# A tuned convolution and feed-forward kernel: softmax pieces, bands and second matmuls of blocks 1 to 4 in another order, with the next block's convolution sooner

## The chip, the cores and the metric

The kernel runs on one core of a Trainium2 chip. The metric is device time in microseconds (us), the median of several executions. All runs told of here were in the fast state, with a granted TensorE clock (the share of full speed) of 0.998 to 1.0. Ratios are the mean time of one kernel's fast runs over the mean of the other's in the same rounds on the same chip, so they are not quite the ratio of the medians quoted; the interval beside a ratio is the 95% one.

## The reference, cut to what matters

```python
def _attn_ref(x, weight_gen):                       # x (8, 4096, 192), weight_gen (8, 4096, 8, 7)
    w = np.exp(weight_gen - max over the 7 taps);  w = w / sum over the 7 taps
    # each position and head: weighted sum of the 7 last positions of x (a causal convolution)
    return np.einsum('bshk,bskhg->bshg', w, x_unfolded).reshape(8, 4096, 192)

def _moe_ref(x, w_in, w_out):                       # x (32768, 192), w_in (192, 2048), w_out (2048, 192)
    h = np.maximum(x @ w_in, 0.0)
    return h * h @ w_out
```

The convolution's result is the input of the feed-forward part.

## The kernel before

The 32768 rows are worked through in blocks: blocks 0 and 1 have 512 rows, all others 1024. A string for each block, its plan, gives the order in which work is issued. One letter is one step:

- `u`, a unit: 6 matmuls of the first product into an h tile (PSUM), a relu on ScalarE into a t1 tile, a square on VectorE into a g tile. A block of 1024 rows has 16.
- `M`, one half of one quarter of the second product: 32 matmuls into the two o banks. The second half of a quarter is followed by a copy of one bank on ScalarE and an add of the other on VectorE.
- `C`, the convolution of the next block: 120 short matmuls into two h tiles, then two copies on ScalarE (y).
- `E`, `S`, `B`: an exp on ScalarE, a softmax piece on VectorE (total, reciprocal, four scalings), and a band on VectorE (a masked spread of the weights that the conv's matmuls read). The last piece of a part also issues the transfers that carry its rows to the bands. `L` loads weights.

```python
p_t1 = ctx.enter_context(tc.tile_pool(name="p_t1", bufs=5))
ps_h = ctx.enter_context(tc.tile_pool(name="ps_h", bufs=3, space=bass.MemoryType.PSUM))
ps_o = ctx.enter_context(tc.tile_pool(name="ps_o", bufs=1, space=bass.MemoryType.PSUM))
...
def st_unit(j, u):
    h = ps_h.tile([P, 2, TB], f32, name="h", tag="h")
    ...                                              # 6 matmuls
    t1 = p_t1.tile([P, 2, TB], f16, name="t1")
    nc.scalar.activation(out=t1, in_=h, func=ActF.Relu)
    g = p_g.tile([P, 2, TB], f16, name="g")
    nc.vector.tensor_tensor(out=g, in0=t1, in1=t1, op=AluOp.mult)
...
def st_conv(j):
    yps = [ps_h.tile([P, 2 * TB], f32, name="yp", tag="h") for _ in range(-(-NK // per))]
    ...                                              # 120 matmuls
...
def o_sum(j, qt, ccs, o):
    nc.scalar.copy(out=o_sb, in_=o[0][:, c])
    if len(o) == 2:
        nc.vector.tensor_tensor(out=o_sb, in0=o[1][:, c], in1=o_sb, op=AluOp.add)
...
steady = "MuMuuu" * 3 + "MuuuMCu"
plans = {
    0: "B1 X1 u u u E1 S1 u C u u u u",
    1: "L3 u u B2 M E2 B3 u M E2 u u S2 u M u C u S2 M",
    2: "L4 u u u E3 M u u u M B4 u u u u M B5 S3 u u u u M u E3 C u",
    3: "L5 L6 M S3 u u u M u u u u M u M B6 E4 u u u M M B7 u u S4 u E4 M u C M u",
}                                                    # from block 4 on: steady, with E, S, B filled in
```

The program issues work to every engine in this order, and the traces show it done in it: in the run with M C u below, ScalarE's copy was done at 75.90 us, and the add on VectorE that follows it began only at 77.83, after the softmax piece and the squares issued ahead of it. So a step's place fixes what stands ahead of it in each engine's queue. An h tile is one of 3, which the conv shares; a t1 tile is one of 5; the two o banks are there once.

The softmax here doesn't subtract the row's maximum and nothing guards it: scores larger than these inputs give would overflow.

## Time and profile before

| | before |
|---|---|
| median | 748.29 us (747.95 to 749.56, 4 runs); first measured as 748.35 (3 runs) |
| span of the traced run | 746.6 us |
| TensorE busy | 739.0 us |
| ScalarE, VectorE busy | 624.7, 621.8 us |
| matmuls | 15,106, each with its own weight load |

The busy line, the chain that ended last and the one wait of TensorE stand in the prediction below. Three more lines of the page are needed. The first is from the list of transfer queues (packets, MB, share of the 16 transfer engines' time), the others are the two costliest groups of matmuls (count, busy us, mean ns, then the idle time ahead of them and what ended it):

```profile
q8 instruction: 118, 1.93, 1.1%
...
L475 PE MATMUL o<-w_o,g 64*128 64x192 f16 (+1 forms) x8032 | 385.3, 243 | 0.9 <-DVE o_sb L491 0.6
...
L441 PE MATMUL h<-y,w_i 64*128 64x512 f16 (+1 forms) x3168 | 379.7, 370 | 2.2 <-ACT t L450 0.9
```

### The profile page before, as it was taken

To read this page: it belongs to the slowest core of one execution; us is meant where nothing else is said; L and a number is where in the kernel's file an instruction comes from. 1 tells how busy PE (TensorE), PEld (TensorE's weight loads), DVE (VectorE), ACT (ScalarE), POOL (GpSimd) and SP (SyncE) were. 2 spreads that over 40 slices of the span, in tenths; PEclk is the share of its full clock that TensorE was granted. 3 is DMA by queue.
4 is the path that set the end of the run, shared out by engine and by line. 5 is a ranking of instruction groups with operands and counts; after the bars stand their busy time and mean duration, and the time that the engine had idled before them with its cause. 6 is when DMAs were issued, how large, how long until landed. Compare 5 with 4: busy or idle time off the path is not lost.

```text
span 746.6 us, 33289 instructions
## 1 busy us (share of the span) xinstructions
PE 739.0 (99%) x15106; PEld 556.5 (75%) x15106; DVE 621.8 (83%) x1001; ACT 624.7 (84%) x755; POOL 88.8 (12%) x130
## 2 busy tenths in 40 slices
PE   8999999999999999999999999999999999999998
PEld 4767877877777777777777777787777777777787
DVE  5999998998889888888889888898888987677853
ACT  5998788888888888888888888888888888888874
POOL 7321220101101100011000110001100011001000
PEclk9999999999999999999999999999999999999999
DMA  8654454436554234644245542365441354441312
GB/s 223 112 106 109 80 101 85 100 70 139 94 118 79 75 57 80 140 79 73 45 74 139 102 65 53 51 139 108 59 80 48 57 108 80 60 73 51 51 46 65
DMA packets 122169, 64.81 MB, mean 87 GB/s; under 512 B 83849, under 2 KB 118636, under 8 KB 121516
## 3 DMA queue, kind: packets, MB, share of 16 engines
q1 hardware_dynamic: 77708, 45.66, 22.4%
q0 software_dynamic: 44176, 16.93, 20.5%
q8 instruction: 118, 1.93, 1.1%
q14 instruction: 23, 0.19, 0.1%
q10 hardware_dynamic: 144, 0.10, 0.0%
HBM read 48.61 MB, written 28.70 MB: 104 GB/s over the span
## 4 chain that ended last, share of the span: by engine, by line
PE 94%; DVE 2%; issue 1%; DMA 1%; ACT 1%; POOL 0%; DVEq 0%; ACTq 0%
PE o L475 45%; PE h L441 43%; PE yp L416 6%; DVE g L453 1%; DVE bd L348 1%; DMA wr<-v_first 0%; DMA wg<-in_weight_gen_dram 0%; POOL wr L330 0%; ACT t L450 0%; DVE v_first L239 0%; ACT ex L217 0%; DVE ssum L224 0%; DVE rcp L231 0%; DVE o_sb L491 0%; ACT y L427 0%
## 5 line engine op out<-in xcount | busy, mean ns | idle before, releaser
L450 ACT ACTIVATE t<-h 128x1024 f16<-128x1024 f32 x512 | 496.7, 1026 | 65.6 <-PE h L441 65.3
L453 DVE TENSOR_TENSOR g<-t 128x1024 f16<-128x1024 f16 x512 | 334.3, 687 | 100.5 <-ACT t L450 97.8
L475 PEld LDWEIGHTS <-g 64*128 64x128 f16 (+1 forms) x8032 | 352.3, 94 | 55.0 <-issue 4.8
L475 PE MATMUL o<-w_o,g 64*128 64x192 f16 (+1 forms) x8032 | 385.3, 243 | 0.9 <-DVE o_sb L491 0.6
L441 PE MATMUL h<-y,w_i 64*128 64x512 f16 (+1 forms) x3168 | 379.7, 370 | 2.2 <-ACT t L450 0.9
L441 PEld LDWEIGHTS <-w_i 64*128 64x128 f16 x3168 | 162.6, 94 | 117.2 <-issue 5.2
L348 DVE TENSOR_TENSOR bd<-wr,mask 128x4160 f16<-128x4160 f16 (+3 forms) x89 | 149.3, 1701 | 4.0 <-DMA wr<-v_first 4.0
L300 POOL DMA_DIRECT2D xt<-in_x_dram x62 | 51.2, 830 | 446.7 <-PE yp L416 423.7
L489 ACT COPY o_sb<-o 128x384 f32<-128x384 f32 x129 | 62.2, 482 | 33.8 <-PE o L475 33.8
L491 DVE TENSOR_TENSOR o_sb<-o,o_sb 128x384 f32<-128x384 f32 x123 | 68.2, 555 | 8.4 <-ACT o_sb L489 5.6
L427 ACT CAST y<-yp 128x1024 f16<-128x1024 f32 (+1 forms) x64 | 48.1, 803 | 14.5 <-PE yp L416 14.5
L416 PE MATMUL yp<-bd,xt 128*32 128x104 f16 (+8 forms) x3864 | 51.7, 208 | 0.3 <-DVE bd L348 0.2
L416 PEld LDWEIGHTS <-xt 128*32 128x32 f16 (+3 forms) x3864 | 46.2, 92 | 6.7 <-issue 6.2
L239 DVE TENSOR_TENSOR v_big<-ex,rcp 128x112 f16<-128x112 f32 (+1 forms) x136 | 27.3, 263 | 1.8 <-DMA vd<-v_big 0.6
L217 ACT ACTIVATE ex<-wg 128x448 f32<-128x448 f32 (+2 forms) x44 | 27.2, 618 | 1.8 <-DMA wg<-in_weight_gen_dram 1.8
L224 DVE TENSOR_REDUCE ssum<-ex 128x64 f32<-128x448 f32 (+2 forms) x44 | 26.1, 594 | 2.5 <-ACT ex L217 2.3
L231 DVE RECIPROCAL rcp<-ssum 128x64 f32<-128x64 f32 (+2 forms) x44 | 23.7, 539 | 1.5
L290 POOL DMA_DIRECT2D xt<-in_x_dram x7 | 3.8, 549 | 135.8 <-PE yp L416 135.8
L330 POOL DMA_DIRECT2D wr<-v_first x31 | 16.8, 561 | 16.3 <-DVE v_first L239 16.1
L539 PE MATMUL wp<-warm 128*128 128x512 f16 x39 | 11.4, 459 | 1.3 <-DVE warm L531 1.3
L539 PEld LDWEIGHTS <-warm 128*128 128x128 f16 x39 | 4.3, 114 | 7.6 <-issue 3.5
L239 DVE TENSOR_TENSOR v_first<-ex,rcp 128x112 f16<-128x112 f32 (+1 forms) x48 | 9.1, 255 | 0.3
(24 smaller groups left out, 28.2 us busy)
## 6 DMA issues: line engine op xcount, KB each, us to landing
out_dram<-o_sb SPq DMA_DIRECT2D x63, 384.0 KB, 3.0
xt<-in_x_dram POOLq DMA_DIRECT2D x42, 240.0 KB, 5.9
wg<-in_weight_gen_dram SPq DMA_DIRECT2D x4, 1064.0 KB, 8.3
xt<-in_x_dram POOLq DMA_DIRECT2D x20, 192.0 KB, 5.6
wr<-vd SPq DMA_DIRECT2D x38, 80.0 KB, 3.6
vd<-v_big SPq DMA_DIRECT2D x5, 512.0 KB, 5.5
wg<-in_weight_gen_dram SPq DMA_DIRECT2D x5, 392.0 KB
wg<-in_weight_gen_dram SPq DMA_DIRECT2D x3, 616.0 KB, 4.1
```

What stands on the lines that cost most here:

```text
L217: nc.scalar.activation(out=self.ex[:, lo:hi].rearrange("p r g k e -> p (r g) k e"), in_=self.wg[:, lo:hi].rearrange("p r (g e) k -> p (r g ...
L239: eng.tensor_tensor(out=bass.AP(tensor=v.tensor, offset=v.offset + lo * H * SL + lo % SL * 2 + g * SL * 2, ap=[list(v.ap[0]), [H * SL + 2, ...
L300: eng.dma_start(out=dst[:, first:last], in_=ap)
L348: nc.vector.tensor_tensor(out=bd_t[j][:, H * lo : H * (lo + len(tiles) * n)].rearrange("p (g m c) -> p g m c", g=shape[1], c=2 * SL), in0= ...
L416: nc.tensor.matmul(out=yps[k // per][p0 : p0 + m, col + a : col + b], lhsT=x_t[s][:, i, 32 * q : 32 * q + m], rhs=bd[:, h // 2, h % 2, a - ...
L427: nc.scalar.copy(out=y[:, k0:k1, 0:th], in_=yp[:, 0 : (k1 - k0) * th].rearrange("p (k c) -> p k c", c=th),)
L441: nc.tensor.matmul(out=h[:, half, jj * th : (jj + 1) * th], lhsT=w_in_chunk(u * per + jj, slot, half), rhs=y_t[j][r0 : r0 + RT, k, 0:th], ...
L450: nc.scalar.activation(out=t1, in_=h, func=ActF.Relu)
L453: nc.vector.tensor_tensor(out=g, in0=t1, in1=t1, op=AluOp.mult)
L475: nc.tensor.matmul(out=oo[:, cc * Dm : (cc + 1) * Dm], lhsT=g[r0 : r0 + n, cc * P : (cc + 1) * P], rhs=w_o[r0 : r0 + n, fc, :], start=(fc ...
L489: nc.scalar.copy(out=o_sb, in_=o[0][:, c])
L491: nc.vector.tensor_tensor(out=o_sb, in0=o[1][:, c], in1=o_sb, op=AluOp.add)
```

## The change

As the plans read, it moves softmax pieces and bands to other places in VectorE's order, moves the conv of the next block up in block 3, and spreads the halves of the second product around them. Plans 1 to 3 are rewritten, and block 4 gets a plan of its own. Nothing else changes; the set of instructions is the same.

```diff
-            1: "L3 u u B2 M E2 B3 u M E2 u u S2 u M u C u S2 M",
-            2: "L4 u u u E3 M u u u M B4 u u u u M B5 S3 u u u u M u E3 C u",
-            3: "L5 L6 M S3 u u u M u u u u M u M B6 E4 u u u M M B7 u u S4 u E4 M u C M u",
+            1: "L3 u u B2 M E2 B3 u M E2 u u S2 u M u S2 C u M",
+            2: "L4 u u u E3 S3 u B4 u B5 M E3 u u S3 M u u u M u u u u M u C M u",
+            3: "L5 L6 u u u M E4 B6 u u u M u M E4 B7 u u u M M S4 C S4 u M u u u M u u",
+            4: "B8 u E6 M u M S6 u u u u M u u M u B9 E5 u u M M u C M u u E5 u M S5 u",
```

## The prediction

Passages of the record are cut where marked: rules that it had not measured, and the hand-over times that it put beside the copy and the add. No term of its sum is among them; the sum came to +1.3, that is 749.6. Its 1.25 us for copy and add is an estimate: the trace of before shows 0.48 and 0.55, with 0.03 us from the last matmul's end to the copy, 0.03 from the copy to the add and 0.05 from the add to the next matmul, 1.14 in all. That a busy TensorE need not be at its pace shows in the same trace: it is busy for all of 36.8 to 56.3 us, and three units there take 2.05 us (from 36.82) against 1.94 later (from 56.27). That the 3 h tiles and 5 t1 tiles are "just" enough in the steady blocks is its judgement; the trace shows that TensorE waits for no engine from 150 to 740 us.

> **What bounds the kernel now.** I read the page first (busy shares, then the chain that ended last), then the TensorE timeline block by block, then who waited for whom between 24 and 150 us, then the timelines of VectorE (DVE) and ScalarE (ACT) for the blocks that change.

> The page's busy line and the chain's shares:
> ```profile
> PE 739.0 (99%) x15106; PEld 556.5 (75%) x15106; DVE 621.8 (83%) x1001; ACT 624.7 (84%) x755; POOL 88.8 (12%) x130
> PE 94%; DVE 2%; issue 1%; DMA 1%; ACT 1%; POOL 0%; DVEq 0%; ACTq 0%
> ```
> TensorE ends the run. A busy PE need not be at its pace, so I took start-to-start distances. From about 55 us on, one unit (st_unit, 6 matmuls) takes 0.65 us and one half of a second matmul (an "M" of the plan, 32 matmuls) 1.32 us, again and again; a conv ("C") takes 1.53 us. The last stretch of block 3 and the start of block 4, TensorE timeline (start, length, engine, group, count, idle before it):
> ```profile
> 73.99 1.59 PE L416 MATMUL yp<-bd,xt 128*32 128x104 f16 x120
> 75.52 1.49 PE L475 MATMUL o<-w_o,g 64*128 64x192 f16 x32
> 76.85 0.81 PE L441 MATMUL h<-y,w_i 64*128 64x512 f16 x6
> 77.57 0.24 PE L475 MATMUL o<-w_o,g 64*128 64x192 f16 x1
> 78.43 1.48 PE L475 MATMUL o<-w_o,g 64*128 64x192 f16 x31 [0.62 <-DVE o_sb L491]
> ```
> This is the one visible hole. Block 3 ends "M C M u" and block 4 begins with "M": only one unit stands between the half that finishes a quarter of the output and the half that starts the next quarter in the same two o banks. The second matmul should have started near 77.61 and starts at 78.43: 0.82 us lost. In the list of waits of 24 to 150 us it is the only wait of PE on another engine:
> ```profile
> PE o L475 <- DVE o_sb L491: 0.6, 1, 0.6
> ```
> Other losses in these blocks are small: the first M of block 5 takes 1.43 us to the next start instead of 1.32, and a half at 139.3 us takes 1.62, together 0.4. They are in block 5, which the diff doesn't touch. The plan of the change adds no instruction and drops none (16 units and 2 bands a block, the same exps, softmax pieces and halves in total), so **all that can be gained is about 0.8 us, perhaps 1.2, of 748**.

> [...]at 77.04 the copy of the o bank starts on ACT and takes 0.48, so the add on DVE could start at about 77.55, but it stands behind two squares (g) and starts at 77.83. So the place of each piece in the queue is what the change plays with. [...]The trace's 99% hides the pace, but it is constant. [...]in the steady blocks there are none (PE has no wait on another engine from 150 us to 740), so the rings of 3 h tiles and 5 t1 tiles are just enough there. Whether they are enough in the new block 2 is the question below.

> **The change part by part.** Durations from the VectorE and ScalarE timelines of before, as start-to-start steps: g 0.60, a softmax piece of 8 rows 1.99 (total 0.61, recip 0.55, four scales 0.83), one of 6 rows 1.65, a band 2.23 to 2.27, an add 0.47; on ACT a relu (t1) 0.91, an exp 0.54, a copy of o 0.45, the two y copies together 1.4. VectorE in block 1 to 2 before:
> ```profile
> 37.94 0.50 DVE L224 TENSOR_REDUCE ssum<-ex 128x48 f32<-128x336 f32 x1
> 39.59 1.89 DVE L453 TENSOR_TENSOR g<-t 128x1024 f16<-128x1024 f16 x3
> 42.28 0.69 DVE L453 TENSOR_TENSOR g<-t 128x1024 f16<-128x1024 f16 x1 [0.80 <-ACT t L450]
> 44.72 2.32 DVE L348 TENSOR_TENSOR bd<-wr,mask 128x4160 f16<-128x4160 f16 x1
> 49.36 2.35 DVE L348 TENSOR_TENSOR bd<-wr,mask 128x3328 f16<-128x3328 f16 x2
> 57.28 0.49 DVE L224 TENSOR_REDUCE ssum<-ex 128x48 f32<-128x336 f32 x1
> ```
> VectorE has 1.2 us to spare at 42 to 44 and then none until after 58.9.

> (1) Boundary of blocks 3 and 4. After the change one half of block 2's quarters moves into block 2 and block 3 ends "M u u", block 4 begins "u E6 M": three units, 1.94 us, instead of one. The copy [...] and the add [...] need about 1.25. **Saved: 0.82.**

> (2) Block 2. Both pieces S3 and both bands now stand within the first 7 units. TensorE's order starts at 36.82 as before. VectorE from 36.14, back to back: g, g 1.2; S2 1.65; g 0.6; three g 1.8; S3 1.99; g 0.6; B4 2.23; g 0.6; B5 2.27; then g of unit 6, 0.6: 13.54, so that this g ends at 49.7. The relu of unit 11 takes its t1 buffer (5 of them) and can't start before 49.7; unhindered it would start at about 48.85 (unit 11 ends at 36.82 + 5 units 3.35 + M 1.43 + 2 units 1.40 + M 1.43 + 3 units 2.05 + M 1.43 + 0.75 = 48.66). Its h buffer is then free at 50.75 and unit 14, which needs it, is due at 50.1. **Lost: about 0.7** (0.2 to 1.1, as the sum of 13.54 has small gaps either way and the band may wait for its rows). The rest of the block has room: second S3 piece ends at 52.0, relu 13 waits for a g of 52.5, just in time for the conv.

> (3) Block 3 and most of block 4. With adds at the head of the bands, each gap between a finishing half and the next starting half is two units and a conv or three units (1.94 to 2.2), and the ledger leaves 0.4 to 1.0 of margin at each: lost 0, up to 0.3. The conv five units sooner in block 3 gains nothing: conv is 1.53 us of TensorE wherever it stands, and its y was never waited for in the steady blocks.

> (4) Boundary of blocks 4 and 5. The new block 4 ends "C M u u E5 u M S5 u", and block 5 begins with "M". **This is the pattern of the old boundary 3/4 again**, one unit in between; the old block 4 ended "M C u" there, with 2.2 us. From the conv's start as zero: unit 13 is done at 3.6; ACT does relu 13 from 3.75, relu 14, exp (0.54), relu 15, to 7.0, then the copy to 7.4; TensorE has finished the half at 6.25 and wants the o banks at 6.87. The g of unit 15 (0.6) and the add (0.55) bring it to 8.2. **Lost: about 1.3** (0.6 if ACT and DVE are not behind, since copy and add alone need 1.25 against 0.65).

> (5) Behind it, S5's two pieces and S6 come within 6 us on VectorE in block 5; margin of the next add about 0: lost 0 to 0.2, say 0.1.

> Sum: -0.8 + 0.7 + 0 + 1.3 + 0.1 = +1.3, that is 749.6. I give some weight to the rivals and put it at 749.2.

> **Rivals.** First, the author's hope: the hole at 78.4 goes and nothing takes its place, 747.4. For it: that hole is the only recorded wait of PE; the total work is the same. Against: block 4's new end repeats the pattern, and the VectorE timeline shows no slack after 44 us in block 2. Second, only the hole moves (0.8 at 78 becomes 0.6 to 1.3 at the 4/5 boundary) and block 2 keeps pace: 748.1 to 748.9. For it: the five t1 buffers have carried a lag of some 3 us on VectorE before. Third, the pile-up in block 2 is worse: B4 and B5 also wait for the rows that S2 moves (before, issued from 39.7 and first read at 44.7; now both some 0.7 sooner), TensorE loses 1.5 in block 2, and the lag meets the adds in block 3: 750.5. For it: VectorE has 19.8 us of work in 20 us of block 2. Against: every lag of TensorE lets VectorE catch up, so it can't grow without end.

> **Range and chances.** The terms run from -0.8 + 0 + 0.6 = -0.2 to -0.8 + 1.1 + 0.3 + 1.4 + 0.2 = +2.2 about the median of 748.35, and the three times of before themselves spread by 1.3. So 747.6 to 750.6. Two per cent are 15 us, ten times any term: within 2% is all but certain.

> **What would show it.** Right: the TensorE timeline of after has no hole at the 3/4 boundary (about 79 us), a hole of 0.6 to 1.4 released by the DVE add at the first half of block 5 (about 102 us), and in block 2 (near 50 us) a unit that starts 0.2 to 1.1 late after a relu; all blocks from 6 on take as long as before. Wrong: no hole at 102, which would mean that ACT and DVE are further ahead at the end of block 4 than my ledger has them; or no delay in block 2; or a wait on a transfer, which I have at zero. A time under 747.5 would mean that the first rival holds; one over 751 that a lag carried through block 3 into several adds.

## The result

| | before | after |
|---|---|---|
| median | 748.29 us (4 runs) | 752.51 us (4 runs, 752.40 to 753.29) |
| ratio | | 1.0056 (1.0038 to 1.0073) |
| span of the traced run | 746.6 us | 750.7 us |
| matmul 566, early in block 2 | 37.27 us | 38.33 us |
| from there to matmul 2300 (called blocks 2 to 5; 2300 lies in block 5) | 88.47 us | 92.49 us |
| from there to matmul 15,000 | 611.82 us | 610.92 us |

The change costs 4.2 us. That is within 2%, as foretold, but outside the range of 747.6 to 750.6. The last three rows are worked out from the start times of matmuls with the same number, counted from 0, in both traces.

The busy line and the chain's shares of the page after:

```profile
PE 739.2 (98%) x15106; PEld 562.1 (75%) x15106; DVE 621.8 (83%) x1001; ACT 624.2 (83%) x755; POOL 90.7 (12%) x130
PE 90%; DVE 5%; DMA 1%; ACT 1%; issue 1%; POOL 0%; DVEq 0%; ACTq 0%
```

All engines have the same work. TensorE's part of the chain falls from 94 to 90%, VectorE's rises from 2 to 5%: TensorE has to wait. Its timeline after (start, length, engine, group, count, idle before it and what ended it), with the three new holes and the place where the old one was:

```profile
49.22 2.12 PE L441 MATMUL h<-y,w_i 64*128 64x512 f16 x18
52.56 0.82 PE L441 MATMUL h<-y,w_i 64*128 64x512 f16 x6 [1.22 <-ACT t L450]
...
55.49 1.58 PE L416 MATMUL yp<-bd,xt 128*32 128x104 f16 x120
57.00 1.32 PE L475 MATMUL o<-w_o,g 64*128 64x192 f16 x27
59.42 0.42 PE L475 MATMUL o<-w_o,g 64*128 64x192 f16 x5 [1.10 <-DVE g L453]
...
80.72 2.18 PE L441 MATMUL h<-y,w_i 64*128 64x512 f16 x18
82.66 1.56 PE L475 MATMUL o<-w_o,g 64*128 64x192 f16 x32
...
103.99 0.81 PE L441 MATMUL h<-y,w_i 64*128 64x512 f16 x6
105.25 0.24 PE L475 MATMUL o<-w_o,g 64*128 64x192 f16 x1 [0.45 <-ACT o_sb L489]
106.08 1.48 PE L475 MATMUL o<-w_o,g 64*128 64x192 f16 x31 [0.58 <-DVE o_sb L491]
```

- **Unit 14 of block 2** starts at 52.56, 1.38 us late (the distance between two matmuls, less the usual one; so are all losses below).
- **The half behind block 2's conv** stops after 27 of its 32 matmuls and goes on at 59.42, 1.30 us late. The prediction has nothing like it.
- **The boundary of blocks 3 and 4** is clean: three units in 1.94 us, then the half. The old hole of 0.81 is gone.
- **The start of block 5** has two holes, 0.61 and 0.78 us, for the two o banks.

Two smaller losses: 0.25 us at the fifth of the five units with which block 2 now begins, and 0.47 us in the half behind block 3's conv, again after its 27th matmul. The sum is 1.38 + 1.30 + 0.61 + 0.78 + 0.25 + 0.47 - 0.81 = 3.98, close to the 4.02 us by which blocks 2 to 5 grew. The 1.06 us at the start is tested below. The 0.90 won back later did not come again: in the second trace of the same code the last stretch took 612.85 us.

The list of waits for 24 to 150 us puts names to the holes:

```profile
PE h L441 <- ACT t L450: 1.2, 1, 1.2
PE o L475 <- DVE g L453: 1.1, 1, 1.1
...
PE o L475 <- DVE o_sb L491: 0.6, 1, 0.6
...
PE o L475 <- ACT o_sb L489: 0.5, 1, 0.5
```

For the hole before unit 14, VectorE's and ScalarE's timelines show what is behind it. VectorE:

```profile
43.01 0.61 DVE L224 TENSOR_REDUCE ssum<-ex 128x64 f32<-128x448 f32 x1
...
45.60 2.32 DVE L348 TENSOR_TENSOR bd<-wr,mask 128x4160 f16<-128x4160 f16 x1
...
48.43 2.35 DVE L348 TENSOR_TENSOR bd<-wr,mask 128x3328 f16<-128x3328 f16 x2
50.70 1.28 DVE L453 TENSOR_TENSOR g<-t 128x1024 f16<-128x1024 f16 x2
51.91 0.49 DVE L224 TENSOR_REDUCE ssum<-ex 128x48 f32<-128x336 f32 x1
```

ScalarE:

```profile
46.61 3.02 ACT L450 ACTIVATE t<-h 128x1024 f16<-128x1024 f32 x3
51.48 1.94 ACT L450 ACTIVATE t<-h 128x1024 f16<-128x1024 f32 x2 [1.85 <-DVE g L453]
54.33 1.94 ACT L450 ACTIVATE t<-h 128x1024 f16<-128x1024 f32 x2 [0.91 <-DVE g L453]
```

A softmax piece, square, band, square, band: only at 50.70 come the squares of units 6 and 7. The relu of unit 11 waits for the first of them to free its t1 tile, starts at 51.48, and unit 14 starts when it is done. By 58.45 VectorE has caught up; it then idles for 3.13 us, until 61.58.

For the stop at 59.42 the list names a square on VectorE. That looks wrong: the half reads the squares of units 1 to 8, and the eighth was done at about 54.2. Nor does a stop after 27 matmuls fit a square: each square is read by 4 matmuls of the half, so a wait for one would fall after 24 or 28. With the matmuls and their weight loads numbered in order, both 27-matmul stops of the trace, though a conv and some hundreds of instructions apart, lie at the same place of 256. Worked out from the trace's records:

```
stop at    number in stream   of 256   last packet of queue 8   TensorE goes on
 58.09          1726            190      56.69 to 57.97 us       59.42, 1.45 after it landed
 76.76          2494            190      74.63 to 75.78 us       77.28, 1.49 after it landed
```

So the theory to test was: in these two places TensorE had run out of instructions.

### The profile page after: what moved, and what is told of

Same layout as the page of the kernel before. It is cut to its first block, busy times and chain, and to the rows that moved or that the text cites. A ratio compares the mean times of both kernels' runs of the same rounds, so it can differ in the third digit from the quotient of the medians.

```text
span 750.7 us, 33286 instructions
## 1 busy us (share of the span) xinstructions
PE 739.2 (98%) x15106; PEld 562.1 (75%) x15106; DVE 621.8 (83%) x1001; ACT 624.2 (83%) x755; POOL 90.7 (12%) x130
## 4 chain that ended last, share of the span: by engine, by line
PE 90%; DVE 5%; DMA 1%; ACT 1%; issue 1%; POOL 0%; DVEq 0%; ACTq 0%
PE o L475 43%; PE h L441 41%; PE yp L416 6%; DVE g L453 2%; DVE bd L348 1%; DMA wr<-v_first 1%; DVE v_first L239 1%; ACT t L450 1%; DVE ssum L224 1%; DVE rcp L231 1%; DMA wg<-in_weight_gen_dram 0%; ACT ex L217 0%; POOL wr L330 0%; DVE o_sb L491 0%; ACT y L427 0%
## 5 line engine op out<-in xcount | busy, mean ns | idle before, releaser
L450 ACT ACTIVATE t<-h 128x1024 f16<-128x1024 f32 x512 | 497.1, 1027 | 69.6 <-PE h L441 66.5
L453 DVE TENSOR_TENSOR g<-t 128x1024 f16<-128x1024 f16 x512 | 334.7, 688 | 103.8 <-ACT t L450 101.2
L475 PEld LDWEIGHTS <-g 64*128 64x128 f16 (+1 forms) x8032 | 352.1, 94 | 56.3 <-issue 6.7
L475 PE MATMUL o<-w_o,g 64*128 64x192 f16 (+1 forms) x8032 | 384.6, 243 | 2.6 <-DVE g L453 1.1
L441 PE MATMUL h<-y,w_i 64*128 64x512 f16 (+1 forms) x3168 | 378.5, 370 | 3.4 <-ACT t L450 2.1
L441 PEld LDWEIGHTS <-w_i 64*128 64x128 f16 x3168 | 167.3, 94 | 113.4 <-issue 6.8
L348 DVE TENSOR_TENSOR bd<-wr,mask 128x4160 f16<-128x4160 f16 (+3 forms) x89 | 149.3, 1703 | 4.7 <-DMA wr<-v_first 4.7
L491 DVE TENSOR_TENSOR o_sb<-o,o_sb 128x384 f32<-128x384 f32 x123 | 68.2, 555 | 8.2 <-ACT o_sb L489 5.6
L416 PE MATMUL yp<-bd,xt 128*32 128x104 f16 (+8 forms) x3864 | 51.6, 208 | 0.4 <-DVE bd L348 0.3
L416 PEld LDWEIGHTS <-xt 128*32 128x32 f16 (+3 forms) x3864 | 46.1, 91 | 6.8 <-issue 6.5
L224 DVE TENSOR_REDUCE ssum<-ex 128x64 f32<-128x448 f32 (+2 forms) x44 | 26.1, 594 | 2.6 <-ACT ex L217 2.5
```

Of the source, the lines that this page charges most:

```text
L224: nc.vector.tensor_reduce(out=self.ssum[:, lo:hi].rearrange("p r g e -> p (r g) e"), in_=self.ex[:, lo:hi].rearrange("p r g k e -> p (r g) ...
L348: nc.vector.tensor_tensor(out=bd_t[j][:, H * lo : H * (lo + len(tiles) * n)].rearrange("p (g m c) -> p g m c", g=shape[1], c=2 * SL), in0= ...
L416: nc.tensor.matmul(out=yps[k // per][p0 : p0 + m, col + a : col + b], lhsT=x_t[s][:, i, 32 * q : 32 * q + m], rhs=bd[:, h // 2, h % 2, a - ...
L441: nc.tensor.matmul(out=h[:, half, jj * th : (jj + 1) * th], lhsT=w_in_chunk(u * per + jj, slot, half), rhs=y_t[j][r0 : r0 + RT, k, 0:th], ...
L475: nc.tensor.matmul(out=oo[:, cc * Dm : (cc + 1) * Dm], lhsT=g[r0 : r0 + n, cc * P : (cc + 1) * P], rhs=w_o[r0 : r0 + n, fc, :], start=(fc ...
```

## The experiments

Theories. **A**: the hole before unit 14 is VectorE's pile of S3, B4, B5 acting through the 5 t1 tiles. **B**: the 27-matmul stops are want of instructions; rival: they are waits for squares. **C**: the holes at block 5's start are the copy and add in one unit's time; rival: ScalarE and VectorE lag there anyway. **D**: the 1.06 us at the start is chance; rival: the change makes it.

All twelve runs and the two kernels in one table, the holes from one trace each. "Unit 14" and "27th" are the losses in us at the two places in block 2, "packet" the start of the queue 8 packet relative to the conv of block 2, "relu 13" the end of unit 13's relu relative to it (the conv's first matmuls take that unit's h tile), "ends" the hole at the boundary that the kernel has one at.

| run | median | ratio (95%) | blocks 2-5 | unit 14 | 27th | packet | relu 13 | ends |
|---|---|---|---|---|---|---|---|---|
| before | 748.29 | | 88.47 | 0 | - | +0.23 | -1.16 | 0.81 (3/4) |
| after | 752.51 | 1.0056 (1.0038-1.0073) | 92.49 | 1.38 | 1.30 | +1.20 | -0.13 | 1.39 (4/5) |
| after, again | 752.37 | 1.0049 (1.0034-1.0064) | 91.86 | 0.83 | 1.54 | +1.14 | -0.13 | 1.40 (4/5) |
| 8 t1 tiles | 749.64 | 1.0016 (1.0000-1.0032) | 89.96 | 0 | 0.47 | +0.88 | -1.16 | 1.40 (4/5) |
| end of block 4 | 752.71 | 1.0051 (1.0035-1.0068) | 92.37 | 0.87 | 1.09 | +1.20 | -0.13 | 2.09 (in 5) |
| stream shifted | 750.84 | 1.0030 (1.0015-1.0045) | 91.26 | 1.48 | 0 | - | -0.14 | 1.39 (4/5) |
| half put back | 750.91 | 1.0037 (1.0023-1.0051) | 91.07 | 0.86 | 0 | +1.16 | -0.13 | 1.39 (4/5) |
| three repairs | 748.57 | 1.0006 (0.9994-1.0019) | 88.67 | 0 | 0 | +0.38 | -1.16 | 0.39 (in 5) |
| before, M C u | 749.30 | 1.0014 (1.0001-1.0026) | 88.92 | 0 | - | +0.25 | -1.16 | 0.90 (3/4) |
| before, half moved | 749.20 | 1.0015 (1.0000-1.0031) | 88.80 | 0 | 0.25 | +0.29 | -1.16 | 0.80 (3/4) |
| S3 later | 750.28 | 1.0025 (1.0012-1.0038) | 90.94 | 0.82 | 0.34 | +0.33 | -1.15 | 1.39 (4/5) |
| before, B6 sooner | 749.25 | 1.0013 (1.0000-1.0026) | 89.21 | 0 | - | +0.34 | -1.16 | 0.85 (in 3), 0.83 (3/4) |
| order alone | 748.22 | 0.9997 (0.9985-1.0009) | 88.64 | 0 | 0 | +0.54 | -0.57 | 0.39 (in 5) |
| last try | 749.47 | 1.0010 (0.9996-1.0024) | 88.31 | 0 | 0.29 | +0.44 | -1.16 | 0 |

### The changed kernel again

No edit.

> The changed kernel once more. In its first trace the matmuls of the start-up run 1.05 us later than in the trace of before from the 68th matmul on, although the order of work up to there is the same in both. If that is chance of a run (when the first small transfers land), a second trace starts block 2 at another time than 37.88 us, anywhere from 36.8 to 38.2. If the change causes it, it is 37.9 again, within 0.1. In both cases the holes come again at the same matmuls: about 1.4 us before unit 14 of block 2, 1.3 us after the 27th matmul of the half after block 2's conv, 0.5 us after the 27th of the half after block 3's conv, and 0.6 + 0.8 us at the first two matmuls of block 5. Time 752.5.

Measured: block 2 began 0.84 us sooner than in the first trace, and the time was the same, 752.37. Over all fourteen traces matmul 566 starts anywhere between 37.2 and 38.8 us: at 37.27 to 37.99 in the four that have plans 0 and 1 of before, at 37.2 to 38.8 in the ten that have the changed ones. So D holds as far as these traces show: the 1.06 us is chance. In the first trace of the changed kernel VectorE's first band waited for its rows until 12.62 us, in that of before until 11.57; why that varies stays open. The holes are at the same matmuls. The stop behind the conv is there again with 1.54 us, and here the timeline gives another releaser for it:

```profile
58.27 0.42 PE L475 MATMUL o<-w_o,g 64*128 64x192 f16 x5 [1.33 <-issue]
```

"Issue" means that it waited for nothing that the profile shows. So the square in the first trace was only the event that came last before it: VectorE's last square ended at 58.45, 0.97 us before TensorE went on. The hole before unit 14 was 0.83 in place of 1.38: in the first trace a band of block 1 had waited 0.47 us for its rows, and VectorE's whole pile stood that much later.

### 8 t1 tiles

```diff
-    p_t1 = ctx.enter_context(tc.tile_pool(name="p_t1", bufs=5))
+    p_t1 = ctx.enter_context(tc.tile_pool(name="p_t1", bufs=8))
```

> The changed kernel with 8 t1 buffers in place of 5. Theory: unit 14 of block 2 waits for an h buffer, its relu waits for a t1 buffer, and that one waits for a square on VectorE behind S3, B4 and B5. Then with 8 buffers the relus of units 11 to 13 run at once and the 1.4 us before unit 14 go (under 0.2 left); the time falls by about 1.4. Rival: the exp E3 and the copies put ScalarE itself behind; then the hole stays at 1 us or more with 8 buffers. The three other holes stay under both.

TensorE's timeline of this run, from unit 11 on:

```profile
49.69 2.76 PE L441 MATMUL h<-y,w_i 64*128 64x512 f16 x24
...
54.56 1.62 PE L416 MATMUL yp<-bd,xt 128*32 128x104 f16 x120
56.11 1.33 PE L475 MATMUL o<-w_o,g 64*128 64x192 f16 x27
57.71 0.42 PE L475 MATMUL o<-w_o,g 64*128 64x192 f16 x5 [0.27 <-issue]
```

Four units run through in 2.76 us; the hole is gone, with VectorE's order untouched. A holds. The expectation was wrong in one thing: the other holes should have stayed, but the 27-matmul stop fell to 0.47, and the time by 2.7 us, not 1.4 (its trace shows 1.9 us of it in blocks 2 to 5). The two holes hang together.

### The end of block 4

```diff
-            4: "... B9 E5 u u M M u C M u u E5 u M S5 u",
+            4: "... B9 E5 u u M M u C M u M u E5 u S5 u",
```

> The changed kernel with the end of block 4's plan M u u E5 u M S5 u made M u M u E5 u S5 u, so that two units more stand between the last half of block 4 and the first of block 5. Theory: the 1.4 us at the first two matmuls of block 5 are the copy and the add of the output in the one unit between these halves; they go, and the time falls by 1.2 to 1.4. Rival: VectorE and ScalarE are behind at this place anyway (exp and softmax piece); then 0.5 us or more stay at the start of block 5. The other holes stay.

Measured: the holes at the first half of block 5 went, and others came, 1.53 us in the second half and 0.56 in the third; blocks 2 to 5 took as long as before this edit. TensorE's timeline:

```profile
105.36 1.32 PE L475 MATMUL o<-w_o,g 64*128 64x192 f16 x28
108.01 0.34 PE L475 MATMUL o<-w_o,g 64*128 64x192 f16 x4 [1.33 <-DVE g L453]
```

This stop comes after 28 matmuls, at 120 of 256, and is a true wait: the last 4 matmuls need the square of block 4's last unit, which VectorE did from 107.27, behind the softmax piece S5. So the rival of C has the better part of it: one unit's time (0.65 us) is too short for copy (0.48) and add (0.55), but with two units more VectorE's lag came out in the second and third half of block 5 (1.53 and 0.56 us).

### The instruction stream shifted

```diff
-                nc.tensor.matmul(out=wp, lhsT=warm[:, 0:P], rhs=warm, start=True, stop=True)
+                for c in range(0, TB, TB // k):     # k = 2 for the 25 first: 50 of 256 columns
+                    nc.tensor.matmul(out=wp[:, c : c + TB // k], lhsT=warm[:, 0:P],
+                                     rhs=warm[:, c : c + TB // k], start=True, stop=True)
```

> The changed kernel with the 25 warm-up matmuls of 512 columns made 50 of 256: [...]50 more TensorE instructions ahead of all others, so that what follows lies 50 places later in TensorE's instruction stream. Theory: the half after block 2's conv stops after its 27th matmul for want of instructions, as its next one begins a new block of 256 (both stops lie at 193 of 256 in the stream). Then the stop moves away from that matmul, and as the border now comes while slower parts run ahead of it, it shrinks from 1.3 us to under 0.3; the stop in block 3 moves as well, to the first matmuls of the half. Rival: it is a wait for a square on VectorE, as the wait list has it: then it stays at the 28th matmul with 1.3 us. Time 751.2 under the theory, 752.5 under the rival.

TensorE's timeline at the same place:

```profile
51.54 0.82 PE L441 MATMUL h<-y,w_i 64*128 64x512 f16 x6 [1.32 <-ACT t L450]
...
54.48 1.58 PE L416 MATMUL yp<-bd,xt 128*32 128x104 f16 x120
55.99 1.50 PE L475 MATMUL o<-w_o,g 64*128 64x192 f16 x32
```

The half runs through. Nothing was done to any square, buffer or order; only 50 instructions were put in at the start. In their place came a stop of 0.44 us after block 4's conv, again at number 190 of 256. The rival of B falls. (The 193 of the expectation is the 190 of the table above, counted otherwise. The hole before unit 14, 1.48, and those at block 5 stayed, so the time is only 1.5 us lower.) In all fourteen traces together, every loss of over 0.14 us at 190 of 256, some sixty of them, ends 1.2 to 1.6 us after a packet of queue 8 has landed. All of them stand within 40 matmuls behind a conv. And if the packets are taken in order, one for each such place, TensorE passed none of the 1,638 places, with or without a stop, sooner than 1.2 us after its packet had landed; each packet started when TensorE was 66 to 296 instructions short of its place.

### The half put back

```diff
-            2: "... M u u u u M u C M u",     3: "L5 L6 u u u M E4 B6 ..."
+            2: "... M u u u u M u C u",       3: "L5 L6 M u u u M E4 B6 ..."
```

> The changed kernel with the half that it moved to directly behind block 2's conv put back behind the last unit, at the head of block 3, as before the change. Theory: TensorE runs out of instructions because a conv (240 instructions in 1.5 us) and a half (64 in 1.3 us) without a unit between use up a fetched block of 256 sooner than the next one comes; with the unit (12 instructions in 0.65 us) first, the same border comes 0.65 us later. Then the 1.3 us (0.9 to 1.5 in the four traces so far) shrink to 0.4 to 0.9 and stay at row 190 of 256; time 751.6 to 752. Rival: it is nothing but the lateness of that packet; then all goes with a packet in time and nothing changes with a late one. The hole before unit 14 and those at block 5 stay.

Measured: no stop in the half, though the packet was late, +1.16. Neither side had that: unit 16, now right behind the conv, lost 0.61 us to the relu of unit 15, and in that time the packet came. The time fell by 1.5 us. So the position of the half matters, but this run doesn't separate it from the packet's lateness.

### Three repairs at once

8 t1 tiles, the half put back, and another end of block 4.

```diff
-    p_t1 = ctx.enter_context(tc.tile_pool(name="p_t1", bufs=5))
+    p_t1 = ctx.enter_context(tc.tile_pool(name="p_t1", bufs=8))
-            2: "... u u u u M u C M u",            3: "L5 L6 u u u M E4 B6 ..."
-            4: "... B9 E5 u u M M u C M u u E5 u M S5 u"
+            2: "... u u u u M u C u",              3: "L5 L6 M u u u M E4 B6 ..."
+            4: "... B9 E5 u u M M u C S5 M u M u E5 u u"
```

> The changed kernel with three repairs at once: 8 t1 buffers, the half put back behind block 2's last unit, and block 4's end made C S5 M u M u E5 u u, which gives two units between the last half and the next and also takes the softmax piece S5 out of the way of block 4's last square (in the run with the end alone repaired that square kept the second half of block 5 waiting 1.5 us). If these three holes are all that the change costs, the time is that of before less the hole that it did remove, 747.4; with what is left of want of instructions in block 2 and 3 (0.2 to 0.5 each), 747.6 to 748.2. Rival: new holes come up elsewhere, as in that run, and it stays above 749.5.

Measured: 748.57 us, ratio 1.0006, and blocks 2 to 5 in 88.67 us, 3.8 and 3.2 less than the two traces of the changed kernel. So these places are what the change costs. It does not beat before: 0.51 us of want of instructions behind block 3's conv, 0.39 in block 5 and 0.25 at block 2's start are left.

### Before with one edit: M C u

```diff
-            3: "... B7 u u S4 u E4 M u C M u",
+            3: "... B7 u u S4 u E4 M u M C u",
```

> The kernel before with one edit: block 3 ends M u M C u in place of M u C M u, so that the conv stands between the last half of block 3 and the first of block 4, as in the steady plan. Theory: the only wait of TensorE on another engine in the trace of before (0.8 us at 77.6) is the copy and add of the output in one unit's time; it goes and nothing takes its place: ratio to before 0.999, 747.5. Rival: VectorE's lag behind bands and softmax shows at another place in block 3, or the conv next to a half starves TensorE of instructions as it does in the changed kernel; then 748.2 or more.

Measured: the hole stayed, 0.90 us, although 2.2 us now lie between the two halves. VectorE's add in this run:

```profile
77.83 0.55 DVE L491 TENSOR_TENSOR o_sb<-o,o_sb 128x384 f32<-128x384 f32 x1
```

It starts at 77.83, to the hundredth as in before, though ScalarE's copy was done at 75.90. VectorE is busy without a gap from 66 us on. The old hole was never for want of a conv between the halves; it was VectorE's lag behind B6, B7 and S4.

### Before with one part of the change: the half behind the conv

```diff
-            2: "... M u E3 C u",      3: "L5 L6 M S3 u u u ..."
+            2: "... M u E3 C M u",    3: "L5 L6 S3 u u u ..."
```

> The kernel before with one part of the change alone: the first half of block 2's output moved from the head of block 3 to directly behind the conv of block 2. The softmax pieces, bands and everything on VectorE stay. If the stop after the 27th matmul of that half comes from the half standing directly behind the conv, it is there with about 1 us or more and the time grows by 1. If it also needs the late packet of instructions, which in the changed kernel starts 0.9 to 1.2 us after the conv's start and in before 0.2, the stop is 0 to 0.3 us here and the time is that of before within 0.4. In both cases the hole at the boundary of blocks 3 and 4 stays.

Measured: the packet started 0.29 us after the conv did, and the stop was 0.25 us. So with a packet in time the half's place costs a quarter of a microsecond in this trace; the rest of the 1.30 to 1.54 goes with the late packet. (The time of 749.20 is more than the expected 748.7; its trace shows 0.3 us of the 0.9 in blocks 2 to 5 and 0.7 at the start.)

### The second softmax piece of block 2 later

```diff
-            2: "... u B5 M E3 u u S3 M u u u M u u u u M u C M u",
+            2: "... u B5 M E3 u u M u u u M S3 u u u u M u C M u",
```

> The changed kernel with one edit: the second softmax piece S3 of block 2 stands behind the third half in place of ahead of the second. The square of unit 6, which unit 11's relu waits for, is ahead of S3 in both, so the hole before unit 14 stays (0.8 to 1.4 us). But the square of unit 8 now ends some 1.7 us sooner, so that the relu of unit 13, whose buffer the conv's first matmul takes, ends about 1.1 us before the conv in place of 0.13. Theory: [...]the packet of instructions starts 0.2 to 0.5 us after the conv's start in place of 1.1 to 1.2, and the stop after the half's 27th matmul shrinks from 0.9 to 1.5 us to under 0.5. Rival: the packet is late because of the hole itself; then it stays at 1.1 to 1.2 us and the stop at 0.9 or more. Time 751.2 under the theory, 752.3 under the rival.

TensorE's timeline:

```profile
51.28 0.82 PE L441 MATMUL h<-y,w_i 64*128 64x512 f16 x6 [0.66 <-ACT t L450]
...
55.73 1.88 PE L475 MATMUL o<-w_o,g 64*128 64x192 f16 x32
```

The hole before unit 14 is there, 0.82, and the half behind the conv loses 0.34 (1.64 us to the next start) in place of 1.3. The packet started at +0.33. Both are within what the theory said: the packet's lateness goes not with the hole but with the relu of unit 13, which ends 0.13 us before the conv when S3 stands ahead of the square it needs, and 1.15 before it here. The table bears it out: relu at -1.16, packet at +0.23 to +0.44; at -0.57, +0.54; at -0.13, +1.14 to +1.20. So the packet starts 1.1 to 1.6 us after that relu ends, in twelve of the thirteen traces that have a packet there. The one with 8 t1 tiles is off (-1.16 and +0.88), and I can't say why. Why the packet goes with that relu no run shows.

### Before with B6 sooner and M C u

```diff
-            3: "L5 L6 M S3 u u u M u u u u M u M B6 E4 u u u M M B7 u u S4 u E4 M u C M u",
+            3: "L5 L6 M S3 u u u M u u u u M B6 u M E4 u u u M M B7 u u S4 u E4 M u M C u",
```

> The kernel before with two edits in block 3: band B6 one unit sooner (VectorE has idle bits of 0.2 to 0.5 us ahead of it), and M C u at the end as in the run before. In that run the hole at the boundary of blocks 3 and 4 stayed at 0.9 us: the add stood behind VectorE's bands and softmax piece, and started at 77.8 whether the conv came before or after the last half. If it is VectorE's lag, starting B6 some 1.2 us sooner starts the add that much sooner: the hole falls below 0.2 and blocks 2 to 5 take 87.7 us against 88.5. Rival: something else on VectorE moves into its place, and it stays at 0.5 or more. Time 747.5 to 747.9, or 748.3 under the rival.

Measured: the rival. The band now stood ahead of a square that an add had to follow, TensorE lost 0.85 us there, and 0.83 at the boundary as ever; blocks 2 to 5 took 89.21.

### Repaired by order alone

```diff
-            2: "... S3 u B4 u B5 M E3 u u S3 M u u u M u u u u M u C M u",
-            3: "L5 L6 u u u M E4 B6 ..."
-            4: "... M M u C M u u E5 u M S5 u"
+            2: "... S3 u B4 u M E3 u u B5 M u u u M S3 u u u u M u C u",
+            3: "L5 L6 M u u u M E4 B6 ..."
+            4: "... M M u C S5 M u M u E5 u u"
```

> The changed kernel repaired by order alone, with 5 t1 buffers: in block 2 band B5 stands behind unit 7 and the second S3 behind the third half, the half behind block 2's conv goes back to the head of block 3, and block 4 ends C S5 M u M u E5 u u. If the hole before unit 14 is VectorE's pile of S3, B4, B5 and S3 ahead of the squares of units 6 to 8, it goes without more buffers, under 0.2; blocks 2 to 5 take as long as with 8 buffers, 88.7 us within 0.4, against 92.5 in the changed kernel and 88.5 in before. Time 748.2 to 748.9. Rival: without the buffers a part of the hole stays, and the time is over 749.3.

Measured: 748.22 us, ratio 0.9997 (0.9985 to 1.0009). Five moves of one step each (B5, one S3, one half of block 2, and S5 and a half in block 4) take back all that the change cost, with 5 t1 tiles. It is level with before, not better.

### A last try to beat both

On top of that order: 8 t1 tiles, block 3's conv followed by two units, and both pieces of S5 behind block 4's conv (the second came at the start of block 5). The matching edit of the table of softmax times is left out here. The lines stand against the run before:

```diff
-    p_t1 = ctx.enter_context(tc.tile_pool(name="p_t1", bufs=5))
+    p_t1 = ctx.enter_context(tc.tile_pool(name="p_t1", bufs=8))
-            3: "... S4 C S4 u M u u u M u u",    4: "... M M u C S5 M u M u E5 u u"
+            3: "... S4 C S4 u u M u u M u u",    4: "... M M E5 u C S5 S5 M u M u u u"
```

> The order repaired as in the run before, with the three holes that its trace still shows in blocks 2 to 5 treated too: 8 t1 buffers (0.3 us at block 2's last unit, which waits for a late relu), one unit more between block 3's conv and the next half (0.3 us of want of instructions at row 190), and both pieces of S5 in the 3.6 us in which VectorE idles behind block 4's conv (0.4 us in block 5, where a half waits for the add behind S5). If these are separate and nothing comes in their place, blocks 2 to 5 take 87.6 us against 88.6 in the run before and 88.5 in before, and the time is 747.2 to 747.6, ratio 0.9985 to 0.999. Rival: as in the runs with one hole mended alone, others take their place: 748.0 or more.

Measured: 749.47 us against 748.84 for before on that chip, ratio 1.0010 (0.9996 to 1.0024); blocks 2 to 5 in 88.31. The hole in block 5 is below the 0.14 us counted and the one at the conv of block 3 down to 0.14; but the start of block 2 came at 38.6 us and the stretch after block 5 took 1.7 us more than in the run before, most of it at later borders of instruction blocks (190 of 256). The gain that was left is smaller than these swings, and no kernel tried is shown to beat before.

## Why the prediction was wrong

- **What bounds the kernel** held: the instructions are the same, TensorE's pace sets the end, and the gain was at most 0.8 us.
- **Part (1)**, 0.82 saved: came about, 0.81. Its reason was half wrong, so the number is in part luck. In before the add was late by VectorE's lag, not by the one unit's time; the run with M C u shows it.
- **Part (2)**, 0.7 lost before unit 14: the mechanism was right (more t1 tiles, or other places for B5 and the second S3, take it away), and the size 0.82 to 1.48 in the six traces that have it. The pile of 13.54 us took 13.63; where a band of block 1 waits for its rows, it begins later. The 0.25 us at the fifth of five units in a row was overlooked.
- **Part (3)**, nothing lost to adds: right as to the adds. But **the step that failed** is here: the cost of the conv as "1.53 us of TensorE wherever it stands", and with it the line at the end that puts "a wait on a transfer" at zero. Part (2) rests on it too, where it says that the rest of block 2 has room. A transfer was waited for, by these runs that of TensorE's own instructions: 1.30 and 1.54 us behind block 2's conv and 0.47 and 0.18 behind block 3's. That is 1.77 us of the first trace and 1.72 of the second, more than any other miss. A conv is also 240 instructions in 1.5 us, 160 a microsecond, against 48 in a half and 18 in a unit. With a half directly behind block 2's conv, TensorE stopped in that half for 0.25 to 1.54 us in six traces, until 1.2 to 1.6 us after a packet had landed; in the run with the stream shifted by 50 instructions the half ran through. The page's queue 8 line was in sight and wasn't read. So was a first case: the half of before that took "1.43 us to the next start instead of 1.32" loses it at matmul 2271, 190 of 256, which starts 1.30 us after a packet has landed. (The half of 1.62 us loses its part at 182, which is no border; why stays open.)
- **Part (4)**, 1.3 lost at the boundary of blocks 4 and 5: 1.39. From the conv's start the copy was done after 7.3 us and the add after 8.2, as worked out (7.4 and 8.2).
- **Part (5)**, 0.1 lost: 0.07.
- **The sum** of its own working was +1.3; the parts as they were measured, without the instructions and the fifth unit, come to about +2.0, with them to +4.0 in the first trace and +3.4 in the second. Giving weight to the rivals moved the number from 749.6 to 749.2, away from the truth: all three rivals were about VectorE and the rows. Nor did its sign for a time over 751 hold, a lag carried through block 3 into several adds: in block 3 no add was waited for.

What stays open: why the packet was late in the run with 8 t1 tiles, and why the losses at later borders vary: after matmul 2300 those over 0.05 us sum to 0.6 us in one trace of the changed kernel and to 2.3 in the other. Before with 8 t1 tiles was not run. Nor was it shown why the packet's start goes with the end of unit 13's relu; there are only the packet times above.

## What to carry to other kernels

Where TensorE sets the end, count its instructions per microsecond as well as its time: here 240 instructions of short matmuls in 1.5 us, with a half directly behind them, were followed in six traces by a stop of 0.25 to 1.54 us, which ended 1.2 to 1.6 us after a packet of queue 8 had landed. It was 0.25 to 0.47 where the relu that freed the conv's buffer ended 1.15 us or more before the conv, 1.09 to 1.54 where it ended 0.13 before; with a unit between conv and half it was 0 in three traces and 0.29 in one. When a stop has no plausible releaser, number the instructions: here the same place of 256 each time was the mark of it, and 50 instructions put in far ahead took the stop of 1.30 us away from that half. And a hole that a reorder removes may have been the lag of another engine, as here (0.81 us in before, 0.90 with the conv put between the halves); look for where that lag comes out next before counting the gain.
